# A transformer block on one core: a new head, zero products where TensorE is quiet, reordered waits, and a tail by TensorE transposes

## The chip, the cores and the metric

The kernel runs on one core of one Trainium2 chip. The metric is the device time of one execution, in microseconds (us). Before the change the median was 841.53 us (837.78 to 842.52, four runs). A time in a trace is measured from the start of the profiled execution, whose span is about 2 us shorter than its device time (843.0 us against 844.83 before).

Engines, by the profile's names: PE is TensorE (PEld its weight loads), DVE is VectorE, ACT is ScalarE, POOL is GpSimd, SP is SyncE; SPq lines are DMA issues. PEclk is the granted TensorE clock, 1.00 being full speed.

## The reference

A pre-norm block on 2048 tokens of width 640, in bf16: multi-query attention with 32 heads of width 20 that share one key and one value head, then a gated GELU feed-forward of width 1536.

```python
h  = x + softmax((LN(x) @ wq) @ (LN(x) @ wk).T * 20**-0.5) @ (LN(x) @ wv) @ wo   # 32 heads, one k and v
h2 = h + (gelu(LN(h) @ w_gate) * (LN(h) @ w_up)) @ w_down
```

The costly part is 32 x 2048 x 2048 exponentials. The kernel deals with them in 2048 score banks of 128 x 512.

## The kernel before

Everything is recorded by a planner in Python: tasks have estimated costs and latencies, and at each moment the planner gives each engine something to do. What it decides becomes a fixed order of instructions on every engine, with semaphore waits between engines. A number in the planner changes the order of instructions; it does not change what one instruction does. Both kernels are planned this way, so a small edit can reorder everything after it.

The parts that the argument touches (cut; `...` marks cuts):

```python
# waits of one instruction: DMAs first, then engines, in no order of time
ws = dmas + [v[1] for v in best.values()]
...
# GpSimd at the start, in this fixed order; the LayerNorm powers come after all of it
pool(memset wk4 ...); pool(memset wq_pad[0:4] ...); pool(wk4 copy ...)
for g in range(4): wq_copy(g)          # waits for the first half of wq
... v_ext memsets, ident, memset wq_pad[4:8]
for g in range(4, 8): wq_copy(g)       # waits for the second half of wq
...
# a LayerNorm tile is transposed by DMA, issued by SP
sp_tasks.append(_Task(("sp",), lambda e: e.dma_start_transpose(o, xn_tmp[:, s, :]), 1330, 1500, ...))
...
# the late weight loads (wo, wg, wu, wd): lowest priority, free to go from 30 us of planned time
sp_tasks.append(_Task(("sp",), ... e.dma_start(o[:], cview(v)) ..., [], [nm], 9.0, None,
                      lambda: plan.free["sp"] > 30000.0))
...
# every product has two forms: whole, or split in four pieces of 32 columns
def fn(e, b, mode):
    if mode == "m":
        return e.matmul(o(b), l, r, start=st, stop=sp)
    for j in range(4):
        a = slice(32 * j, 32 * j + 32)
        ins = e.matmul(o(b)[a, :], l[:, a], r, start=st, stop=sp, tile_position=(0, 32 * j))
...
# whole only when no attention unit is open any more
md = "m" if state["qk_left"] == 0 and not open_units() else "v"
...
# PE's choice: PV products go first only under pressure for buffers
if can_v and press:
    return do_pv()
```

A "pack" below is one set of four score products (one key tile for one attention unit); there are 512, and each feeds four score banks. ACT turns most of them into exponentials; DVE does about a quarter by integer arithmetic (545 of the 2048 banks in the profile of before).

The softmax here doesn't subtract the row's maximum and nothing guards it: scores larger than these inputs give would overflow.

Of the kernel before, what the change touches and what calls it, by code (L numbers as in the profile page):

```python
# [9 lines left out]
P = 128  # L10
_DEBUG = {}
# [27 lines left out]
class _Plan:  # L39
# [51 lines left out]
    def resolve(self):  # L91
# [6 lines left out]
        while left:  # L98
            moved = False
            for e in self.ENGINES:  # L100
                while pos[e] < len(self.ops[e]):
# [15 lines left out]
                    for d in need:  # L117
                        if d.dma:
                            dmas.append(d)
                        elif d.idx > best.get(d.eng, (-1, None))[0]:  # L120
                            best[d.eng] = (d.idx, d)
                    ws = dmas + [v[1] for v in best.values()]
                    for d in ws:
# [69 lines left out]
def bass_sequential_preLN__grouped_kv_mqa__glu_gated_geglu__prompt_kernel(  # L193
# [32 lines left out]
    BATCH_COL = [0, 256, 0, 256, 0, 256, 0, 256, 384]  # L226
    LN2G = CHUNKS
    NA = 16
    ND = 8
# [34 lines left out]
    halfc = sb("halfc", [P, 4], BF16)  # L264
    warm = sb("warm", [P, 4], BF16)
    shifts = sb("shifts", [P, 2], I32)
    xn_tmp = sb("xn_tmp", [P, NXT, D], BF16)
# [21 lines left out]
    plan = _Plan()  # L289
    G_ALL = [("g", fc, q) for fc in range(NFC) for q in range(4)]  # L290

# [5 lines left out]

    def c_pe(n, mode):
        return max(n / 2.4, 54.0) + 3.0 if mode == "m" else max(n / 2.4, 90.0) + 9.0

# [7 lines left out]
    ADD_MIN = 1  # L308
    PVF = 4
    PRA = 3  # L310
    PRD = 1
    TH0 = 2500.0
# [3 lines left out]
    MISCMAX = 1500.0  # L316
    L_PE, L_ACT, L_DVE, L_POOL = 250.0, 165.0, 150.0, 100.0

# [18 lines left out]

    pool(lambda e: e.memset(warm[:], 0.0), 80, writes=["warm"])
    pool(lambda e: e.memset(halfc[:], 0.5), 80, writes=["halfc"])
    for w in (1, 2):  # L340
        pool((lambda w: lambda e: e.memset(shifts[:, w - 1:w], CH_SHIFT[w] * 65537))(w), 80, writes=["shifts"])
    pool(lambda e: e.memset(wk4[:].bitcast(F32), 0.0), 330, writes=["wk4z"])
    pool(lambda e: e.memset(wq_pad[:, 0:4, :, :].bitcast(F32), 0.0), 1150, writes=[("wqz", 0)])
    wk4v = wk4[:].rearrange("p c (r e) -> p c r e", r=4)[:, :, :, 0:Dh]
    pool(lambda e: e.tensor_copy(wk4v, wk_sb[:].unsqueeze(2).to_broadcast([P, NC_D, 4, Dh])), 400,
         reads=["wk"], writes=["wk4", "wk4z"])

    def wq_copy(g):
        o = wq_pad[:, g, :, :].rearrange("p c (r e) -> p c r e", r=4)[:, :, :, 0:Dh]
        i = wq_stage[:, :, 4 * Dh * g:4 * Dh * (g + 1)].rearrange("p c (r e) -> p c r e", r=4)  # L350
        pool(lambda e: e.tensor_copy(o, i), 400, reads=[("wqs", g // 4), ("wqz", g // 4)] + G_ALL,
             writes=[("wqp", g)])

    for g in range(4):
        wq_copy(g)
    for w in range(3):
        pool((lambda w: lambda e: e.memset(v_ext[:, :, w, Dh:32], CH_W[w]))(w), 230,
             writes=[("vone", w)])
    plan.commit("act", lambda e: e.activation(warm[:, 0:1], warm[:, 1:2], ACT.Exp), 1500, L_ACT,
# [21 lines left out]

    def ln_stats(ln, t, prio, then):
        key = ("x", t) if ln == 0 else ("h", t)

        def b(op):
            dve(lambda e: e.bn_stats(stats[:, ln, t, 6:12], xh[:, t, HALF:D]), 356, [key], [("st", ln, t, 1)],
                prio, c)

        def c(op):
            dve(lambda e: e.bn_aggr(mv[:, ln, t, :], stats[:, ln, t, :]), 126,  # L390
                [("st", ln, t, 0), ("st", ln, t, 1)], [("mv", ln, t)], prio, then)

        dve(lambda e: e.bn_stats(stats[:, ln, t, 0:6], xh[:, t, 0:HALF]), 356, [key], [("st", ln, t, 0)], prio, b)  # L393

    def ln_group(ln, tiles, prio, done):
# [27 lines left out]
        def norm(t):  # L423
# [9 lines left out]
            def then(op):  # L433
                s = slot[0]

                def tdone(op2):
                    slots["xt"].append(s)
                    done(t, op2)

                if ln == 0:  # L440
                    o = xn1T[:, :, t * P:(t + 1) * P]
                    wkeys = [("xn1T", t)]
                else:
                    o = xn2T[:, :, xcol[t]:xcol[t] + P]
                    wkeys = [("xn2T", xcol[t])]
                def free():
                    return ln == 0 or batch_of[t] < 2 or up_left[batch_of[t] - 2] == 0

                sp_tasks.append(_Task(("sp",), lambda e: e.dma_start_transpose(o, xn_tmp[:, s, :]), 1330, 1500,
                                      [("xt", s)], wkeys, prio, tdone, free))  # L450

            key = ("x", t) if ln == 0 else ("h", t)
            tk = _Task(("dve",), None, 302, L_DVE, [key, ("lr", kk)], [], prio, then, gate)

# [8 lines left out]

        for t in tiles:
            ln_stats(ln, t, prio, after_stats)

# [21 lines left out]
    def mm(o, l, r, st, sp):  # L488

        def fn(e, b, mode):  # L490
# [6 lines left out]
            return ins  # L497
        return fn

    def kv_job(tiles):  # L500
# [157 lines left out]
    def on_transpose(t):  # L658
# [11 lines left out]
        tk.born = bind  # L670
        tk.then = lambda op: wo_job(t, sl[0], 0)
        sp_tasks.append(tk)

    def wo_job(t, s, h):
# [5 lines left out]
        def then(b):  # L680
            if h == 1:
                slots["onT"].append(s)
            else:
                wo_job(t, s, 1)

            def fin(op):
                free_bank(b)
                if h == 1:
                    h_ready(t)
            dve(lambda e: e.tensor_tensor(xh[:, t, h * HALF:(h + 1) * HALF], xh[:, t, h * HALF:(h + 1) * HALF],  # L690
                                          bank(b, HALF), ALU.add), c_dve(HALF), [("b", b), ("x", t)],
                [("hh1", t, h), ("h", t)], 1.0, fin)
        jobs.append(_Job(("wo", t, h), 2.0, pieces, then))

    h_done = set()

    def h_ready(t):
        h_done.add(t)
        for gl in LN2G:
            if t in gl and all(x in h_done for x in gl):  # L700
                ln_group(1, gl, 4.0 if t < 12 else 1.5, x2_done)

# [21 lines left out]

    def g_free(b):

        mine = set(gkeys(b, 0))
        return all(down_left[x] == 0 for x in range(b) if mine & set(gkeys(x, 0)))
# [88 lines left out]
    def down_job(b, t, h):  # L817
# [4 lines left out]
        def then(bk):  # L822
# [4 lines left out]
            def fin(op):  # L827
                free_bank(bk)
                if h == 1:
# [3 lines left out]
                                          bank(bk, HALF), ALU.add), c_dve(HALF),  # L833
                [("b", bk), ("h", t)], [("o", t, h)], 1.0, fin)
        jobs.append(_Job(("down", t, h), 3.0, pieces, then))
# [11 lines left out]
    for i, gl in enumerate([[0], [1], [2, 3], [4, 5], [6, 7], [8, 9], [10, 11], [12, 13], [14, 15]]):  # L847
        ln_group(0, gl, 2.0 + 0.01 * i, ln1_done)
    for u in units:
        q_job(u)  # L850

    pool(lambda e: e.memset(ident[:], 0.0), 120, writes=["ident0"])
    pool(lambda e: e.affine_select(out=ident[:], in_=ident[:], compare_op=ALU.not_equal, fill=1.0, base=0,
                                   pattern=[[-1, P]], channel_multiplier=1), 320, ["ident0"], ["ident"])
    pool(lambda e: e.memset(wq_pad[:, 4:8, :, :].bitcast(F32), 0.0), 1150, writes=[("wqz", 1)])
    for g in range(4, 8):
        wq_copy(g)
    for nm, o, v in (("wo", wo_sb, A_wo), ("wg", wg_sb, B_w_gate), ("wu", wu_sb, B_w_up), ("wd", wd_sb, B_w_down)):
        sp_tasks.append(_Task(("sp",), (lambda o, v: lambda e: e.dma_start(o[:], cview(v)))(o, v), 1500, 12000,
# [255 lines left out]
    def pe_decide(t):  # L1115
# [30 lines left out]
        def fits(c):  # L1146
            return t + c <= lim
# [13 lines left out]
        can_v = nr >= 1 and (fits(220.0 + swv) or press)  # L1161
        can_m = piece is not None and fits(c_pe(piece[1][1], "v") + swv)
        if can_v and press:
            return do_pv()
# [6 lines left out]
        if can_v:  # L1171
            return do_pv()
        return False

    def next_piece(t):
# [52 lines left out]
    def issue_piece(t, jb, pc):  # L1228
# [10 lines left out]
        fn = pc[0]  # L1239
        md = "m" if state["qk_left"] == 0 and not open_units() else "v"  # L1240
        sw = pe_sw(t, md)
# [82 lines left out]
    def do_adds(t, eng, w, most):  # L1324
# [7 lines left out]
        a = slice(s0 * 512, (s0 + k) * 512)  # L1332
        cost, lat = (k * 512 / 3.84 + 72.0, L_DVE) if eng == "dve" else (POOL_ADD, L_POOL)
        if eng == "dve":
            def fn(e):
                return e.tensor_scalar(pd[:, w, a], pd[:, 0, a], float(CH_SHIFT[w]), None, ALU.add)  # L1336
        else:
# [3 lines left out]
            def fn(e):  # L1341
                return e.tensor_tensor(pd32[:, w, h], pd32[:, 0, h],
                                       shifts[:, w - 1:w].to_broadcast([P, 256 * k]), ALU.add)
        op = plan.commit(eng, fn, cost, lat, [("pd", 0, s0 + i) for i in range(k)] + ["shifts"], [("pd", w, s0 + i) for i in range(k)], at=t)
        for x in recs:
            x["add"](w, op)

    def dve_decide(t):
# [52 lines left out]
        if n and pend[w][0]["at"] <= t + 20:  # L1401
# [3 lines left out]
            if n >= 4 or pd_free.count(True) < 3:  # L1405
                pr = 0.2
            if n >= ADD_MIN:
                opts.append((pr, len(opts), None))
# [19 lines left out]

    def pool_decide(t):
        for tk in tasks:  # L1430
            if tk.engs[0] == "pool" and known(tk) and plan.ready("pool", tk.reads, tk.writes) <= t + 20:
                tasks.remove(tk)
                run_task(t, tk, "pool")
                return True
        if POOL_ADD:
# [55 lines left out]
    _DEBUG["end"] = max(op.vis for e in plan.ENGINES for op in plan.ops[e])  # L1491
    _DEBUG["plan"] = plan

    plan.resolve()
# [74 lines left out]
```

## Time and profile before

| | before |
|---|---|
| device time, median | 841.53 us |
| span of the profiled run (another run, of 844.83 us) | 843.0 us |
| first exponential on ACT starts | 24.25 us |
| last exponential ends | 799.28 us |
| tail after it | 43.7 us |

The page's chain of waits that ended last, by line (the beginning is what is used here):

```profile
ACT pa L1301 63%; DVE pd L1364 4%; PE ps L1072 4%; PE ps L993 4%; PE ps L496 4%; DMA xn1T<-xn_tmp 2%; ACT gbuf L797 2%; DVE pd L1336 2%; PE ps L492 1%; DMA onT<-onq 1%; DMA xh<-in_A_x_dram 1%; ACT L1301 1%; ACT L797 1%; DVE stats L393 1%; D
```

ACT's exponentials (line L1301) are 63% of the chain. The stretches view says where they are not the limit. Its columns: the stretch, its length, then for each engine the busy us and (x) instructions, the granted clock, the DMA share and GB/s.

```profile
core 0: us, PE busy (x) PEld busy (x) DVE busy (x) ACT busy (x) POOL busy (x), PEclk, DMA share, GB/s
0.00:24.00 24.00, 4.00 (x120) 3.15 (x120) 16.03 (x65) 2.44 (x5) 13.39 (x34) 1.00 0.71 179
24.00:60.00 36.00, 25.50 (x704) 13.44 (x700) 26.22 (x82) 25.96 (x37) 6.81 (x18) 0.91 0.92 240
60.00:200.00 140.00, 107.74 (x1613) 40.71 (x1609) 128.58 (x330) 134.60 (x191) 0.71 (x1) 0.93 0.04 6
200.00:760.00 560.00, 501.85 (x9679) 233.96 (x9683) 529.50 (x1353) 551.00 (x765) 4.58 (x6) 0.96 0.06 13
799.00:843.00 44.00, 28.59 (x763) 24.13 (x752) 10.89 (x24) 5.74 (x9) 0.56 (x1) 0.92 0.09 25
```

ACT does almost nothing in the first 24 us and the last 44 us, is busy 25.96 of 36 us from 24 to 60, and 134.60 of 140 and 551.00 of 560 us in the bulk. So there are three limits: a head, a bulk bound by ACT with some 15 us of idleness left, and a tail.

Lines of the timeline in the head of before (start us, length us, engine, line, operation, out<-in, count; in brackets idle time before it and what ended it):

```profile
5.16 0.10 DVE L408 TENSOR_SCALAR ln_veb<-ln_vb 128x1 bf16<-128x1 bf16 x1
...
12.10 1.90 POOL L351 COPY wq_pad<-gbuf 128x400 bf16<-128x400 bf16 x4 [1.26 <-DMA gbuf<-in_A_wq_dram]
...
13.97 3.04 POOL L412 TENSOR_TENSOR ln_denb<-ln_veb,halfc 128x1 bf16<-128x1 bf16 x5
...
16.26 0.43 DVE L457 TENSOR_SCALAR xn_tmp<-xh,mv,ln_r 128x640 bf16<-128x640 bf16 x1
...
16.72 16.45 SPq L449 DMA_TRANSPOSE xn1T<-xn_tmp  x12
...
19.46 0.72 PE L496 MATMUL ps<-xn1T,wk 128*32 128x128 bf16 x20 [19.46 <-DMA xn1T<-xn_tmp]
...
24.25 1.94 ACT L1301 ACTIVATE pa<-ps 128x1024 bf16<-128x1024 f32 x2 [0.50 <-PE ps L993]
...
34.61 0.52 SPq L859 DMA_DIRECT2D wg_sb<-in_B_w_gate_dram  x1
38.41 7.76 SPq L449 DMA_TRANSPOSE xn1T<-xn_tmp  x4
...
49.26 1.26 PE L496 MATMUL ps<-xn1T,wk 128*32 128x256 bf16 x20 [1.53 <-DMA xn1T<-xn_tmp]
```

The variance of the first tile is ready at 5.2 us, but its power (L412, on POOL) starts at 13.97, right behind the second set of wq copies (L351). Then the normalised tile (L457), its DMA transpose (L449), and the first key product at 19.46. The last four transposes stand behind one weight load of 1.9 MB (L859), and PE's wait for the last of them ends at 49.26.

Lines of the timeline in the tail of before:

```profile
799.19 2.89 PE L496 MATMUL ps<-wd_sb,gbuf 128*32 128x320 bf16 x80
...
806.49 1.57 PE L496 MATMUL ps<-xn2T,wu_sb 128*32 128x128 bf16 x98 [1.30 <-issue]
...
809.96 0.90 PE L496 MATMUL ps<-xn2T,wg_sb 128*32 128x128 bf16 x50 [1.50 <-issue]
...
813.98 0.33 PE L496 MATMUL ps<-xn2T,wu_sb 128*32 128x128 bf16 x9 [1.70 <-issue]
...
817.51 1.21 SPq L667 DMA_TRANSPOSE onT<-onq  x1
...
820.12 1.53 PE L492 MATMUL ps<-wo_sb,onT 128*128 128x320 bf16 x10 [2.01 <-DMA onT<-onq]
...
825.07 1.21 SPq L449 DMA_TRANSPOSE xn2T<-xn_tmp  x1
...
827.77 4.45 PE L492 MATMUL ps<-xn2T,wg_sb 128*128 128x128 bf16 x40 [6.11 <-DMA xn2T<-xn_tmp]
```

Three stalls of PE are put down to "issue", that is to nothing that the profile shows waiting; they lie where PE runs long rows of 32-column pieces. Then comes the chain of the last tile, with two DMA transposes (L667, L449) that PE waits for.

### The profile page before, as it was taken

What the parts mean: (1) busy time and instruction counts of PE and PEld (TensorE: products, weight loads), DVE (VectorE), ACT (ScalarE), POOL (GpSimd) and SP (SyncE); (2) the same over time, 40 slices, a digit from 0 to 9 for tenths busy, and PEclk for the clock granted to TensorE, in tenths of its full rate; (3) what the DMA queues carried; (4) which work ended last, traced back from release to release, by engine and by line L of the source; (5) the groups of instructions that cost most, each with busy time, mean ns of one, the idle gap of its engine ahead of it and who ended that gap; (6) DMA issues with size and microseconds to landing.
All of it is one profiled execution on the core that took longest, in us unless ns stands there. A gap on an engine that the chain in (4) does not pass through costs nothing.

```text
span 843.0 us, 30901 instructions
## 1 busy us (share of the span) xinstructions
PE 703.7 (83%) x13588; PEld 333.2 (40%) x13588; DVE 748.7 (89%) x1943; ACT 758.7 (90%) x1054; POOL 26.6 (3%) x61
## 2 busy tenths in 40 slices
PE   0777768788997889988997879998998889999965
PEld 0522223243443434443443334344443434444455
DVE  7778998988999989999999899999899999999922
ACT  0769999999999999999999999999999999999910
POOL 5200000000000000000000000000000000000000
PEclk9989899998999999998999989999999999999998
DMA  6980001000010001010010000010010000010010
GB/s 185 193 237 2 2 1 18 9 11 2 3 34 17 3 2 19 19 17 3 2 34 11 9 3 18 2 34 3 2 27 10 18 2 18 10 32 5 11 34 17
DMA packets 42981, 22.68 MB, mean 27 GB/s; under 512 B 34016, under 2 KB 41568, under 8 KB 42848
## 3 DMA queue, kind: packets, MB, share of 16 engines
q1 hardware_dynamic: 40224, 19.83, 10.1%
q8 instruction: 108, 1.77, 0.9%
q10 hardware_dynamic: 2624, 0.87, 0.4%
q14 instruction: 25, 0.20, 0.1%
HBM read 10.21 MB, written 2.62 MB: 15 GB/s over the span
## 4 chain that ended last, share of the span: by engine, by line
ACT 67%; PE 13%; DVE 9%; issue 6%; DMA 5%; SPq 0%; POOLq 0%; POOL 0%
ACT pa L1301 63%; DVE pd L1364 4%; PE ps L1072 4%; PE ps L993 4%; PE ps L496 4%; DMA xn1T<-xn_tmp 2%; ACT gbuf L797 2%; DVE pd L1336 2%; PE ps L492 1%; DMA onT<-onq 1%; DMA xh<-in_A_x_dram 1%; ACT L1301 1%; ACT L797 1%; DVE stats L393 1%; DVE osb L1099 1%
## 5 line engine op out<-in xcount | busy, mean ns | idle before, releaser
L1301 ACT ACTIVATE pa<-ps 128x512 bf16<-128x512 f32 (+1 forms) x1010 | 711.9, 915 | 23.5 <-PE ps L993 21.9
L1364 DVE TENSOR_SCALAR pd<-ps 128x512 uint16<-128x512 f32 x545 | 370.6, 687 | 43.7 <-PE ps L993 32.9
L1072 PE MATMUL ps<-pd,v_ext 128*32 128x512 bf16 x1635 | 276.5, 403 | 30.2 <-ACT pa L1301 14.0
L993 PE MATMUL ps<-qT,kT 32*128 32x512 bf16 x2048 | 208.8, 395 | 61.9 <-ACT pa L1301 29.3
L1072 PE MATMUL ps<-pa,v_ext 128*32 128x512 bf16 x1503 | 253.0, 395 | 5.5 <-DVE pd L1364 2.4
L1336 DVE TENSOR_SCALAR pd<-pd 128x512 uint16<-128x512 uint16 (+2 forms) x895 | 243.8, 312 | 3.0
L993 PEld LDWEIGHTS ps<-qT,kT 32*128 32x128 bf16 x2048 | 58.1, 91 | 222.5 <-DVE pd L1364 176.3
L1072 PEld LDWEIGHTS ps<-pd,v_ext 128*32 128x32 bf16 x1635 | 72.9, 96 | 99.2 <-ACT pa L1301 28.7
L1072 PEld LDWEIGHTS ps<-pa,v_ext 128*32 128x32 bf16 x1503 | 68.4, 96 | 54.1 <-issue 28.8
L496 PE MATMUL ps<-xn2T,wu_sb 128*32 128x256 bf16 (+1 forms) x1920 | 69.6, 276 | 3.8 <-issue 3.0
L496 PE MATMUL ps<-xn2T,wg_sb 128*32 128x256 bf16 (+1 forms) x1920 | 66.5, 271 | 1.7 <-issue 1.5
L496 PE MATMUL ps<-wd_sb,gbuf 128*32 128x320 bf16 x1344 | 58.8, 300 | 0.0
L496 PEld LDWEIGHTS ps<-xn2T,wu_sb 128*32 128x32 bf16 x1920 | 46.3, 99 | 21.7 <-issue 12.6
L496 PE MATMUL ps<-xn1T,wq_pad 128*32 128x256 bf16 (+1 forms) x1440 | 52.3, 276 | 1.6 <-issue 1.1
L814 DVE TENSOR_TENSOR gbuf<-ps,gbuf 128x512 bf16<-128x512 f32 x48 | 32.8, 682 | 21.4 <-PE ps L496 10.8
L496 PEld LDWEIGHTS ps<-xn2T,wg_sb 128*32 128x32 bf16 x1920 | 44.1, 97 | 18.7 <-issue 11.9
L496 PEld LDWEIGHTS ps<-xn1T,wq_pad 128*32 128x32 bf16 x1440 | 33.9, 100 | 15.0 <-issue 8.8
L496 PEld LDWEIGHTS ps<-wd_sb,gbuf 128*32 128x32 bf16 x1344 | 32.2, 96 | 19.1 <-issue 7.5
L412 POOL TENSOR_TENSOR ln_denb<-ln_veb,halfc 128x2 bf16<-128x2 bf16 (+1 forms) x18 | 12.3, 694 | 768.2 <-DVE ln_veb L408 768.2
L777 DVE CAST gbuf<-ps 128x512 bf16<-128x512 f32 x42 | 28.6, 681 | 1.5 <-PE ps L496 1.5
L779 ACT ACTIVATE gbuf<-ps 128x512 bf16<-128x512 f32 x6 | 3.6, 597 | 28.7 <-PE ps L492 19.5
L496 PE MATMUL ps<-wo_sb,onT 128*32 128x320 bf16 x600 | 27.6, 301 | 1.0 <-DMA onT<-onq 0.8
(58 smaller groups left out, 312.6 us busy)
## 6 DMA issues: line engine op xcount, KB each, us to landing
out_dram<-xh SPq DMA_DIRECT2D x16, 160.0 KB, 1.8
xh<-in_A_x_dram SPq DMA_DIRECT2D x3, 640.0 KB, 8.8
wg_sb<-in_B_w_gate_dram SPq DMA_DIRECT2D x1, 1920.0 KB, 10.5
wu_sb<-in_B_w_up_dram SPq DMA_DIRECT2D x1, 1920.0 KB, 8.0
wd_sb<-in_B_w_down_dram SPq DMA_DIRECT2D x1, 1920.0 KB, 13.7
gbuf<-in_A_wq_dram ACTq DMA_DIRECT2D x2, 400.0 KB, 7.5
wo_sb<-in_A_wo_dram SPq DMA_DIRECT2D x1, 800.0 KB, 5.8
xh<-in_A_x_dram SPq DMA_DIRECT2D x2, 160.0 KB, 2.6
```

The costliest lines, as they stand in the source:

```text
L393: dve(lambda e: e.bn_stats(stats[:, ln, t, 0:6], xh[:, t, 0:HALF]), 356, [key], [("st", ln, t, 0)], prio, b)
L412: task(("pool",), lambda e: e.tensor_tensor(ln_denb[:, ln, sl], ln_veb[:, ln, sl], halfc[:, 0:n], ALU.pow), 1010, L_POOL, [("veb", kk), "h ...
L492: return e.matmul(o(b), l, r, start=st, stop=sp)
L496: ins = e.matmul(o(b)[a, :], l[:, a], r, start=st, stop=sp, tile_position=(0, 32 * j))
L777: dve(lambda e: e.tensor_copy(o, i), c_dve(n * k), [("b", bk)], ks, 1.0, fin)
L797: task(("act",), (lambda v: lambda e: e.activation(v, v, ACT.Gelu_apprx_tanh))(v), ("gelu", c_act(n * (f1 - f0))), L_ACT, ks, ks, 1.0, (la ...
L814: dve(lambda e: e.tensor_tensor(o, i, o, ALU.mult), c_dve(n * k), [("b", bk)] + ks, ks, 1.0, fin)
L993: ins = e.matmul(bank(b), kT4[32 * r:32 * r + 32, kt * P:(kt + 1) * P], qT[32 * r:32 * r + 32, s, :], start=True, stop=True, tile_position ...
L1072: ins = e.matmul(ps[32 * r:32 * r + 32, ab * 512:(ab + 1) * 512], v_ext[:, it["kt"], it["w"], :], it["ap"], start=st, stop=(j in ends), ti ...
L1301: op = plan.commit("act", lambda e: e.activation(dst, src, ACT.Exp, scale=SM_SCALE), cost, L_ACT, [("b", b0 + i) for i in range(n)], [("pa ...
L1336: return e.tensor_scalar(pd[:, w, a], pd[:, 0, a], float(CH_SHIFT[w]), None, ALU.add)
L1364: op = plan.commit("dve", lambda e: e.tensor_scalar(pd[:, 0, s * 512:(s + 1) * 512], bank(b), CH_A, CH_B, ALU.mult, ALU.add), c_dve(512), ...
```

## The change

Its intent, by its own words: a new head, with TensorE transposes for the first tiles and GpSimd work by urgency; zero products where TensorE is quiet; the wait that ends last placed last; a tail by TensorE transposes. The diff, cut to its core:

```diff
-                    ws = dmas + [v[1] for v in best.values()]
+                    ws = sorted(dmas + [v[1] for v in best.values()], key=lambda d: d.vis)
...
+    PE_T1 = (0, 1)      # tiles of the first LayerNorm that PE transposes
+    PE_T2 = (15,)       # of the second LayerNorm
+    PE_TO = (15,)       # of the attention output
...
-    PRD = 1
+    PRD = 2
-    L_PE, L_ACT, L_DVE, L_POOL = 250.0, 165.0, 150.0, 100.0
+    L_PE, L_ACT, L_DVE, L_POOL = 232.0, 310.0, 150.0, 100.0
...
-    (fixed order on POOL: wk4 copy, wq copies, v_ext memsets, shifts, ident)
+    (ident first; the copies and memsets become tasks with priorities, as the powers are;
+     the memset of wq_pad[4:8] moves to DVE)
...
+                if t in (PE_T1 if ln == 0 else PE_T2):
+                    tr_job(("tr", ln, t), xn_tmp[:, s, :], ("xt", s), o, wkeys, ...)   # 5 PE transposes, one ACT or DVE copy
+                    return
...
-        if can_v and press:
+        if can_v and (press or state["qk_left"] == 0):
             return do_pv()
...
+        if fits(222.0 + swv) and quiet(t):       # PE planned busy under 50% of the last 3.4 us
+            return fill(t)                       # four products of zeros (32 x 512) into the open accumulator
```

The fills add zero to an accumulator. The order of instructions, which can be built without running, holds 45 of them (180 products), mostly in the first 95 packs. It also shows that in the tail everything after the last PV products now runs in the whole form. Left out of the cut: the statistics of the second LayerNorm are now taken half tile by half tile, and the norm of the last tiles has a higher priority (0.7 instead of 1.5).

## The prediction

> What bounds it now: three stretches with different limits.
> (1) Head. In the timeline the first exponential on ScalarE (ACT) starts at 24.25 us. GpSimd works in fixed order: the first LayerNorm's variance is ready at 5.2 us, but its power starts at 13.97 us, behind eight wq copies (the last four wait for a load) and memsets. The first normalised tile is ready at 16.7 us; its DMA transpose lands 2.74 us later.
> (2) Bulk. ACT is the limit: busy 551 of 560 us from 200 to 760 us (stretches view); the chain of waits is 63% ACT exponentials. From 24 to 799 us ACT idles about 24 us: 10 before 60 us, where TensorE (PE) waits in order for the last DMA transposes among weight loads, 5 from 60 to 200, 9 after.
> (3) Tail. The last exponential ends at 799.3 us: 43.7 us of tail, PE busy only 27.6 of the last 43. From 804 to 814 us PE stalls three times for 1.3 to 1.7 us with no wait for data, about 256 PE instructions apart, in products split into 32-column pieces. [...] From 817.5 to 827.8 us runs the serial chain of the last tile, with two DMA transposes of about 2.7 us; the granted clock falls to 0.79 in 820:830.

> What the change does.
> - Head: the power goes ahead of most wq copies; tiles 0 and 1 are transposed by PE with an ACT copy (estimate 1.4 us, from 0.60 us for 512 columns, instead of 2.7). By instruction order the first norm stands behind the statistics of tiles 2 and 3 (data at 6.55 us): ready at about 9.5 us, second norm 11.5, first query product 12.5, first exponential about 16 us: 8 us earlier. PE reaches the last key products after 15 score packs instead of 11, but VectorE still norms tile 15 at about 41 us, and two transposes now queue behind two 1.9 MB weight loads, so PE waits there until about 47 us (before: 49.3). Four packs at 1.45 us plus 2 us: 7.5 us gained.
> - Bulk: same work (493 paired, 516 single exponentials against 517), 35 fewer VectorE adds (not the bottleneck). Last wait last, a later modelled ACT latency, and 180 zero products (45 sets at 0.2 to 0.4 us, mostly in the first 95 packs) can recover only part of 15 us of ACT idleness, and can delay scores: 3 us gained, give or take 5.
> - Tail: outstanding PV products go first, both units close, and the rest runs as full 128-column products (240 gate/up at 0.064 us = 15.4; 71 down at 0.137 = 9.7; wo 1.5; transposes, PV about 4). PE stays busy; two PE transposes save 1.3 us each and other work fills the chain. Last exponential to end: 32.5 us instead of 43.7, 11 us gained.

> Predicted: 841 - 7.5 - 3 - 11 = 819.5 us; range 810 to 829. Chances: faster by over 2% 0.78, within 2% 0.21, slower 0.01.

> Would show it: first exponential at 15 to 17 us; key wait until 46 to 48 us; ACT at least 98% busy in the bulk, 1.49 us per pack as before; no PE issue gaps after the last exponential, granted clock 1.0 there, tail near 32 us.

> Would make it wrong: the early lead eaten by the wait for tiles 14 and 15; zero products or the new order delaying scores; the tail chain (PV, transpose, wo, LayerNorm) exposed longer than I count; VectorE order stalling PE.

## The result, and the profile after

The changed kernel took 817.96 us (median of four, 817.45 to 822.72), before 841.53 us in the same rounds. The ratio is 0.974, 95% interval 0.969 to 0.979: faster. A ratio here is the mean time of one kernel's runs over the mean of the other's runs of the same rounds, so it is not quite the ratio of the medians. The prediction was 819.5 us, range 810 to 829.

The same stretches after:

```profile
core 0: us, PE busy (x) PEld busy (x) DVE busy (x) ACT busy (x) POOL busy (x), PEclk, DMA share, GB/s
0.00:16.60 16.60, 6.02 (x144) 4.30 (x147) 11.84 (x47) 3.85 (x8) 10.46 (x31) 1.00 0.84 229
16.60:60.00 43.40, 30.03 (x724) 14.18 (x716) 33.43 (x108) 28.92 (x40) 9.11 (x21) 0.84 0.78 203
60.00:200.00 140.00, 112.33 (x1752) 43.02 (x1750) 131.95 (x325) 137.82 (x197) 0.71 (x1) 0.98 0.03 7
200.00:760.00 560.00, 501.40 (x9919) 238.51 (x9919) 533.60 (x1353) 555.09 (x767) 4.61 (x6) 0.98 0.07 13
787.00:816.00 29.00, 25.82 (x339) 22.12 (x337) 11.26 (x24) 6.36 (x10) 0.56 (x1) 0.99 0.07 25
```

From 60 to 200 us ACT is busy 137.82 us (before 134.60), from 200 to 760 us 555.09 (before 551.00), and the granted clock is 0.98 in both (before 0.93 and 0.96). The tail lasts 28.5 us, and PE is busy 25.82 of its 29 us. The head, in lines of the timeline:

```profile
5.37 0.55 POOL L411 TENSOR_TENSOR ln_denb<-ln_veb,halfc 128x1 bf16<-128x1 bf16 x1 [1.21 <-DVE ln_veb L407]
...
9.43 0.39 DVE L460 TENSOR_SCALAR xn_tmp<-xh,mv,ln_r 128x640 bf16<-128x640 bf16 x1
...
9.88 0.71 PE L508 MATMUL ps<-ident,xn_tmp 128*128 128x128 bf16 x5 [9.88 <-DVE xn_tmp L460]
...
16.59 1.94 ACT L1375 ACTIVATE pa<-ps 128x1024 bf16<-128x1024 f32 x2 [0.83 <-PE ps L1037]
...
37.15 0.57 SPq L903 DMA_DIRECT2D wg_sb<-in_B_w_gate_dram  x1
37.77 0.56 SPq L903 DMA_DIRECT2D wu_sb<-in_B_w_up_dram  x1
40.70 7.43 SPq L452 DMA_TRANSPOSE xn1T<-xn_tmp  x2
...
52.59 0.83 PE L498 MATMUL ps<-xn1T,wk 128*32 128x256 bf16 x12 [6.58 <-DMA xn1T<-xn_tmp]
```

The power starts at 5.37 us, PE transposes the first tile (L508) at 9.88, and the first exponential starts at 16.59, 7.7 us earlier than before. But the last two DMA transposes (L452, issued from 40.70) stand behind two weight loads of 1.9 MB (L903), and PE waits 6.58 us for them, until 52.59. The tail:

```profile
787.46 1.67 PE L494 MATMUL ps<-wd_sb,gbuf 128*128 128x320 bf16 x11
...
792.21 1.52 PE L494 MATMUL ps<-wo_sb,onT 128*128 128x320 bf16 x10
...
798.04 0.44 PE L508 MATMUL ps<-ident,xn_tmp 128*128 128x128 bf16 x5
...
800.55 3.42 PE L494 MATMUL ps<-wd_sb,gbuf 128*128 128x320 bf16 x24
```

L494 is the whole form of a product; no row of PE products in the tail carries a gap put down to issue, and none waits for a DMA.

Where the time of the two profiled runs differs, read off the score products and exponentials of both timelines:

| point | before | after | ahead of before |
|---|---|---|---|
| first exponential starts | 24.25 | 16.59 | 7.7 |
| pack 15 starts (counted from 0) | 57.34 | 53.36 | 4.0 |
| pack 24 starts | 69.93 | 66.92 | 3.0 |
| pack 511 (the last) starts | 797.10 | 784.90 | 12.2 |
| last exponential ends | 799.28 | 787.08 | 12.2 |
| end | 843.0 | 815.6 | 27.4 |

So the head keeps 3.0 us of its 7.7, the bulk from pack 24 to 511 gives 9.2 (727.2 to 718.0 us), and the tail 15.2 (43.7 to 28.5). The sum is 27.4 us rather than 23.6, because the profiled run of before is one of its slower ones and the profiled run after is the fastest of its four. That run of before had a granted clock of 0.955; the 30 runs of before have 0.952 to 0.975, and the low clocks go with the long times (848.77 us at 0.952, 837.52 us at 0.975). So part of the 9.2 us belongs to that one run: against a run of before of median length the bulk would have gained nearer 6 us (an estimate, 9.2 less the 3.3 us by which 844.83 is above 841.53, if all of it lies in the bulk).

### The profile page after: what moved, and what is told of

The parts are those of the page before. It is cut to its first block, busy times and chain, and to the rows that moved or that the text cites. A ratio compares the mean times of both kernels' runs of the same rounds, so it can differ in the third digit from the quotient of the medians.

```text
span 815.6 us, 30407 instructions
## 1 busy us (share of the span) xinstructions
PE 700.5 (86%) x13361; PEld 334.7 (41%) x13361; DVE 747.1 (92%) x1913; ACT 759.0 (93%) x1055; POOL 26.0 (3%) x60
## 4 chain that ended last, share of the span: by engine, by line
ACT 67%; PE 20%; DVE 9%; DMA 3%; issue 1%; SPq 0%
ACT pa L1375 64%; PE ps L498 7%; PE ps L1037 5%; PE ps L1116 5%; DVE pd L1438 4%; PE ps L494 3%; ACT gbuf L819 2%; DVE pd L1410 2%; DMA xn1T<-xn_tmp 1%; DVE stats L391 1%; ACT L1375 1%; ACT L819 1%; DVE osb L1143 1%; DMA xh<-in_A_x_dram 1%; DMA onT<-onq 1%
## 5 line engine op out<-in xcount | busy, mean ns | idle before, releaser
L1116 PE MATMUL ps<-pd,v_ext 128*32 128x512 bf16 x1638 | 266.9, 395 | 25.9 <-DVE osb L1143 15.0
L1116 PE MATMUL ps<-pa,v_ext 128*32 128x512 bf16 x1502 | 249.2, 390 | 4.9 <-ACT pa L1375 2.0
L1410 DVE TENSOR_SCALAR pd<-pd 128x512 uint16<-128x512 uint16 (+3 forms) x860 | 239.7, 320 | 2.4
L498 PE MATMUL ps<-xn2T,wu_sb 128*32 128x256 bf16 x1680 | 64.6, 278 | 1.4 <-DVE onq L658 0.7
L498 PE MATMUL ps<-xn2T,wg_sb 128*32 128x256 bf16 x1680 | 62.6, 274 | 0.6 <-DVE onq L658 0.3
L498 PE MATMUL ps<-wd_sb,gbuf 128*32 128x320 bf16 x1252 | 55.2, 300 | 0.2 <-DVE xh L718 0.2
L498 PEld LDWEIGHTS ps<-xn2T,wu_sb 128*32 128x32 bf16 x1680 | 41.3, 97 | 19.7 <-issue 10.0
L498 PE MATMUL ps<-xn1T,wq_pad 128*32 128x256 bf16 (+1 forms) x1440 | 48.7, 266 | 0.3 <-DVE xh L718 0.2
L498 PEld LDWEIGHTS ps<-xn2T,wg_sb 128*32 128x32 bf16 x1680 | 41.3, 96 | 15.3 <-issue 10.5
L391 DVE BATCH_NORM_STATS2 stats<-xh 128x6 f32<-128x320 bf16 x64 | 29.8, 480 | 3.3 <-DMA xh<-in_A_x_dram 3.3
L799 DVE CAST gbuf<-ps 128x512 bf16<-128x512 f32 x42 | 28.6, 682 | 0.0
```

Source lines behind the costliest of these rows:

```text
L391: dve(lambda e: e.bn_stats(stats[:, ln, t, 6 * h:6 * h + 6], xh[:, t, h * HALF:(h + 1) * HALF]), 356, [key], [("st", ln, t, h)], prio, c)
L799: dve(lambda e: e.tensor_copy(o, i), c_dve(n * k), [("b", bk)], ks, 1.0, fin)
L1116: ins = e.matmul(ps[32 * r:32 * r + 32, ab * 512:(ab + 1) * 512], v_ext[:, it["kt"], it["w"], :], it["ap"], start=st, stop=(j in ends), ti ...
L1410: return e.tensor_scalar(pd[:, w, a], pd[:, 0, a], float(CH_SHIFT[w]), None, ALU.add)
```

## The experiments

The theory to test: the head's lead is lost to the order of transposes and weight loads; the bulk gains by the clock that the zero products hold up, and by the order; the tail gains because PV first makes everything whole, which takes away instruction supply stalls. Rivals: the wait order, luck of the order, and the PE transposes.

Twelve kernels ran, four to a chip, each group beside the kernel before. All gave correct results. Five (`waits_old`, `fill_tiny`, `tail_nopv`, `tail_split`, `tail_dma`) leave every instruction's place unchanged up to the point of the edit. The others replan from the head on.

| run | edit to the changed kernel | median us | ratio to before | pack 24 | pack 24 to 511 | tail |
|---|---|---|---|---|---|---|
| again | none | 818.75 | 0.971 | 69.15 | 717.1 | 28.5 |
| waits_old | waits in the old order | 815.39 | 0.967 | 68.70 | 715.1 | 28.6 |
| fill_tiny | zero products of 8 columns | 822.54 | 0.976 | 68.38 | 721.1 | 28.6 |
| null_plan | planner counts 3 ns more | 816.55 | 0.968 | 70.86 | 712.6 | 28.7 |
| tail_nopv | PV not first in the tail | 827.85 | 0.984 | 68.12 | 715.8 | 40.0 |
| tail_split | tail products split | 828.98 | 0.985 | 67.87 | 714.8 | 40.1 |
| tail_dma | last tile by DMA | 819.08 | 0.973 | 68.22 | 717.1 | 28.8 |
| gate_weights | loads after the transposes | 811.24 | 0.964 | 63.10 | 715.3 | 28.6 |
| lat_old | old latencies | 827.14 | 0.982 | 70.15 | 720.0 | 30.3 |
| t1_dma | tiles 0, 1 by DMA | 809.83 | 0.962 | 63.08 | 716.3 | 28.7 |
| pool_fixed | POOL in fixed order | 822.79 | 0.977 | 73.38 | 714.3 | 28.7 |
| gate_waits_old | gate_weights and waits_old | 810.75 | 0.962 | 60.96 | 717.2 | 28.5 |

The last three columns are of each one's profiled run. Pack 24 is the start of that pack; the tail is the span minus the end of the last exponential, good to 0.1 us. Each comparison below with the control (chip 3) is across chips for the second and third group; the ratios to before, taken on one chip, say the same. The three groups, by lines of four, ran on three chips; medians of before there were 841.57, 840.92 and 841.00 us.

| | null_plan | again | after | lat_old | fill_tiny | before |
|---|---|---|---|---|---|---|
| at half clock, us | 3.4 | 17.1 | 23.9 | 27.3 | 37.5 | 61.4 |
| pack 24 to 511, us | 712.6 | 717.1 | 718.0 | 720.0 | 721.1 | 727.2 |

A straight line of 0.25 us for each us at half clock fits all fourteen within 1.3 us. This is a correlation; only fill_tiny, below, shows cause. Five runs that have the instruction order of the changed kernel in this stretch (again, the first profiled run and the three `tail_` runs) spread from 714.8 to 718.0 us, with 10.2 to 23.9 us at half clock, so single reads of the bulk are good to about 3 us.

### again: the control

> The changed kernel itself, as the control of this group. Every theory expects 818 us (first exponential near 16.6 us, last one near 787 us, tail near 28.5 us) and a ratio to before near 0.974; its scatter says how small a difference the other runs can show.

818.17 to 820.72 us in five runs. The first exponential and the tail repeat, but pack 24 came at 69.15 us instead of 66.92: in the profiled run of the same program the wait for the late transposes ended some 2 us later. So single reads of the head are good to about 2 us.

### waits_old: the order of waits

```diff
-                    ws = sorted(dmas + [v[1] for v in best.values()], key=lambda d: d.vis)
+                    ws = dmas + [v[1] for v in best.values()]
```

> Same instructions in the same order on every engine; only the order of the waits before one instruction is put back to that of before. If putting the wait that ends last at the end is worth time (542 of 1057 waiting TensorE instructions wait for two things), the bulk from pack 24 to pack 511 (718.0 us in the changed kernel, 727.2 before) grows by 2 to 4 us. The rival, that a ScalarE which is 98% busy hides it, expects under 1 us of difference.

Neither came: the old order was not slower but 3.4 us faster by medians (814.5 to 818.98 against 818.17 to 820.72, which overlap in one of its six runs). The later pair, gate_waits_old against gate_weights, shows 0.5 us. No gain from putting the last wait last is shown in either pair. Whether it costs anything stays open.

### fill_tiny: zero products without their length

```diff
-  ins = e.matmul(ps[..., ab * 512:(ab + 1) * 512], zz[:], kT4[:, 0:512], start=False, ...)
+  ins = e.matmul(ps[..., ab * 512:ab * 512 + 8],   zz[:], kT4[:, 0:8],   start=False, ...)
```

> Same instructions, order and waits; each zero product has 8 columns instead of 512, so it hardly keeps TensorE busy. If the zero products earn by holding the granted clock, the mean clock falls from 0.977 towards the 0.955 of before, the stretch from pack 24 to 96 (100.5 us changed, 105.4 before) grows back by 3 to 5 us and the total by as much. The rival, that the bulk's gain comes from the new order and the fills do nothing, expects the same time within 1 us; a third, that the fills stand in the way of scores, expects it 1 to 3 us shorter.

822.54 us, with all five runs (821.98 to 825.34) above all five of the control: 3.8 us by medians. The stretches of the control, then of fill_tiny:

```profile
60.00:140.00 80.00, 63.33 (x938) 22.97 (x942) 74.94 (x188) 78.94 (x116) 0.00 (x0) 1.00 0.03 6
400.00:780.00 380.00, 339.61 (x6814) 162.67 (x6813) 363.99 (x916) 378.01 (x523) 4.65 (x5) 0.99 0.08 14
```

```profile
60.00:140.00 80.00, 61.45 (x910) 22.38 (x910) 72.89 (x183) 77.04 (x113) 0.00 (x0) 0.94 0.03 6
400.00:780.00 380.00, 338.58 (x6824) 162.65 (x6817) 364.05 (x917) 378.21 (x523) 4.66 (x5) 0.99 0.08 14
```

Where the fills lie, the clock falls (1.00 to 0.94 from 60 to 140 us) and ACT loses busy time (78.94 to 77.04). From 400 us on, where there are few fills, both are equal. Pack 24 to 511 grew from 717.1 to 721.1 us, and 3.3 us of that lie between packs 24 and 96 (100.5 to 103.8 us, within the expected 3 to 5). The clock theory holds: the fills are worth about 4 us, and all of it in the bulk. The mean granted clock over the profiled run was 0.966, in the control 0.981. Between 60 and 140 us fill_tiny has three stretches of 3.4 us with a granted clock of 0.50 (from 96.2, 113.2 and 123.5 us), the control none. Two long waits of PE show the clock fall while PE stands: in the head of the changed kernel PE stands from 46.01 to 52.59 us, and the clock is at half from 50.6 to 57.5; in the tail of before it stands for 6.11 us until 827.77, and the clock is at half from 825.8 to 832.6. How long a quiet stretch it takes is not shown. What a half clock costs is seen in the head of the changed kernel, where one set of four score products takes 0.61 us at 38.36 us (clock 0.50) and 0.39 us at 41.53 (clock 1.00).

### null_plan: how much a meaningless reordering moves

```diff
-            cost = c_act(512 * n)
+            cost = c_act(512 * n) + 3.0
```

> A meaningless nudge: the kernel's planner counts 3 ns more for each exponential, so the order comes out different from the head on while nothing else is changed. It measures what a different order alone does. If orders are interchangeable, the time stays within 2 us of the control; if it moves by 4 us or more, then the 9.2 us that the bulk gained can be in part luck of the order, and runs that replan from the head on cannot settle differences of that size.

816.55 us, 2.2 us under the control; pack 24 to 511 took 712.6 us, 4.4 less than the control, while pack 24 came 1.7 us later. So a replanned bulk moves by about 4 us for no reason that was meant; it goes with the clock, which was at half for 3.4 us in that stretch instead of 17.1. Differences of that size between replanned runs are not to be put down to the edit.

### tail_nopv: PV not first

```diff
-        if can_v and (press or state["qk_left"] == 0):
+        if can_v and press:
```

> Identical to the changed kernel until the last score product; then outstanding PV products no longer go before other work. The tail (last exponential to end, 28.5 us in the changed kernel, 43.7 before) should grow, as the last unit closes later and more products run split while it is open: by 3 to 8 us if PV first is a main cause of the tail's gain, by under 1 us if the full-width form and the transposes do it all.

The tail grew by 11.5 us (28.5 to 40.0), more than expected, and the total by 9.1 against the control (8.8 against tail_dma on the same chip). The stalls of before are back, three of 1.04 to 1.50 us, and the chain of the last tile is exposed again, because the attention unit stays open while split products go first. By the waits view of its tail PE stands 4.0 us at the stalls and 4.9 us before the transposes and products of that chain.

### tail_split: same order, split products

```diff
-        plan.commit("pe", lambda e: fn(e, b, md), c_pe(pc[1], md) + sw, ...)
+        plan.commit("pe", lambda e: fn(e, b, "v"), c_pe(pc[1], md) + sw, ...)
```

> Same plan, order and waits; in the tail the products of gate, up, down and wo are issued as four 32-column pieces each instead of one full product. If the stalls of 1.3 to 1.7 us every 256 TensorE instructions in the tail of before are instruction supply, they come back: about 310 full products become 1240, about 1860 more instructions with their weight loads, 7 stalls, so the tail grows by 8 to 12 us with idle time put down to issue. If those stalls came from something else, the tail grows by less than 3 us.

The tail grew by 11.6 us, in the expected range of 8 to 12, with nothing moved. The waits view of its tail puts 9.4 us of PE idleness down to issue, in eight stalls. Lines of its timeline:

```profile
809.68 0.41 PE L498 MATMUL ps<-xn2T,wu_sb 128*32 128x128 bf16 x16 [0.22 <-issue]
809.90 1.75 PE L498 MATMUL ps<-xn2T,wg_sb 128*32 128x128 bf16 x112
813.15 0.85 PE L498 MATMUL ps<-xn2T,wg_sb 128*32 128x128 bf16 x48 [1.50 <-issue]
813.82 1.30 PE L498 MATMUL ps<-xn2T,wu_sb 128*32 128x128 bf16 x80
816.62 1.30 PE L498 MATMUL ps<-xn2T,wu_sb 128*32 128x128 bf16 x80 [1.50 <-issue]
```

From the piece at 809.68 to the stall's end at 813.15 PE runs 16 + 112 = 128 products, from there to 816.62 48 + 80 = 128. Each has a weight load, so that is 256 instructions, and each time 3.47 us. In the tail of before the stalls end at 806.49 and 809.96, again 3.47 us apart. From the end of one stall to the next, no 256 instructions took less than 3.47 us here (3.47 to 4.02). The DMA records show what goes with it: queue q8, of kind instruction, moves blocks of 16 KB, and each of the eight stalls here and of the three in the tail of before ends 2.2 to 2.8 us after one of these blocks starts (at 810.88 and 814.32 us for the stalls that end at 813.15 and 816.62). Whole products show no such stall: 20 of them start every 1.12 us, so 128 take 7.2 us, and in the tail of the changed kernel the blocks start at 787.39, 796.41 and 804.86 us, over 8 us apart. That the stalls are waits for the instructions in these blocks is the reading; shown are the equal counts, the blocks before the stalls' ends, and that splitting alone brings the stalls back. The 11.6 us are the price of splitting the whole tail; before paid less of it, three stalls of 4.5 us in all, since from 814.46 us on it ran whole products too.

### tail_dma: the last tile by DMA

```diff
-    PE_T2 = (15,)
-    PE_TO = (15,)
+    PE_T2 = ()
+    PE_TO = ()
```

> Identical to the changed kernel until the tail; the two transposes of the last tile go by DMA again. Counted as a chain they cost 1.3 us more each, so up to 3 us more; if other products fill the wait (as the plan intends), under 1 us; more than 3 us if a DMA also waits behind output stores in its queue.

819.08 us and a tail of 28.8 us, against 818.75 and 28.5: nothing. PE fills the wait with other tiles' products: the waits view of its tail lists no wait of PE for a DMA (its rows go down to 0.7 us). What they are worth where the chain is exposed is not shown: tail_nopv, with PE transposes, has a tail of 40.0 us, and before, without them, one of 43.7, but these two differ in order as well.

### gate_weights: weight loads after the transposes

```diff
-     [], [nm], 9.0, None, lambda: plan.free["sp"] > 30000.0))
+     [], [nm], 9.0, None, lambda: plan.free["sp"] > 30000.0
+                                  and all(("xn1T", t) in plan.w for t in range(NT))))
```

> The three late weight loads are held back until all transposes of the first LayerNorm are issued (replans from 30 us on). In the changed kernel TensorE waits 6.6 us, until 52.6 us, for the transposes of tiles 14 and 15, which were issued behind two weight loads; the lead of 7.7 us at the first exponential is 3.0 us by pack 24. If the loads are what eats the lead, the wait shrinks to under 2 us, pack 24 comes at about 62 to 63 us instead of 66.9, and the total falls by 3 to 5 us. If VectorE's norms are what is late (tile 15 normed at 41.8 us), pack 24 moves by less than 1.5 us.

811.24 us, 7.5 us under the control by medians and 7.8 under tail_dma on the same chip. Pack 24 came at 63.10 us; the three other kernels of that group, which run the changed head, have it at 67.87 to 68.22. SP's lines and PE's last key product in gate_weights:

```profile
12.98 30.93 SPq L452 DMA_TRANSPOSE xn1T<-xn_tmp  x14
43.96 1.56 SPq L903 DMA_DIRECT2D wo_sb<-in_A_wo_dram  x1
45.57 0.53 SPq L903 DMA_DIRECT2D wg_sb<-in_B_w_gate_dram  x1
```

```profile
46.79 1.26 PE L498 MATMUL ps<-xn1T,wk 128*32 128x256 bf16 x20 [1.27 <-DMA xn1T<-xn_tmp]
```

All 14 DMA transposes go out before the first load, and PE's wait for the last is 1.27 us instead of 6.58. The longest time from a transpose's issue to its landing was 4.2 us, in the changed kernel 11.2; tile 15 is normalised no earlier than in the changed kernel (just after 41 us in both). So it is the loads and not DVE that eat the lead. In the trace of the changed kernel the two transposes issued behind 3.8 MB of loads landed just after them: the second load at 51.31 us, the transposes at 51.88 and 52.46. The pack-24 gain is about 5 us; the rest of the 7.5 lies within what replanning moves.

### lat_old: the old latencies

```diff
-    L_PE, L_ACT, L_DVE, L_POOL = 232.0, 310.0, 150.0, 100.0
+    L_PE, L_ACT, L_DVE, L_POOL = 250.0, 165.0, 150.0, 100.0
```

> The changed kernel planned with the latencies of before (TensorE 250, ScalarE 165 ns instead of 232 and 310), so another order from the head on. The zero products account for about 3 us of the bulk's gain (pack 24 to 511: before 727.2, control 717.0, tiny fills 721.3); if the later ScalarE latency is the rest, that stretch grows by 4 to 7 us against the control, beyond the 2 us that the meaningless nudge moved the total. If it is not, the total stays within 3 us of 818.

827.14 us, 8.4 us over the control's median. But in its profiled run, one of 824.59 us, pack 24 to 511 is only 3.0 us longer than in the control, below the expected 4 to 7 and within what null_plan moved by chance; pack 24 comes 1.0 us later and the tail is 1.8 us longer. The total says that in this change the new latencies gave a better order than the old ones, by more than the 2.2 us of the nudge. One nudge does not bound what another order can do by chance (t1_dma, next, moves the total by 8.9 us through an accident of the order), so it is not shown that the latencies themselves are the cause, nor that the bulk's remaining gain is theirs.

### t1_dma: no PE transposes in the head

```diff
-    PE_T1 = (0, 1)
+    PE_T1 = ()
```

> Tiles 0 and 1 are transposed by DMA again. The first exponential moves from 16.6 us to 18.5 to 20 us (a DMA transpose took 2.7 us against 1.6 on TensorE with the copy, and two in a row 1.3 more). If the wait for tiles 14 and 15 swallows the head's lead, pack 24 stays within 67 to 69.5 us and the total within 2 us of 818; if the lead reaches the end, the total grows by 2 to 4 us.

A miss. The first exponential moved to 19.25 us as expected (control 16.81), but the total fell to 809.83 us, 8.9 under the control. In this plan all 16 transposes happen to be issued by 38.06 us, before the first load; pack 24 comes at 63.08 us, as in gate_weights. So this run is in the main the gate again by another road, though not a clean repeat: VectorE's norm of tile 15 also starts earlier, at 33.86 us instead of 41.39. It shows that the PE transposes of the first tiles start the exponentials about 2.4 us earlier. With the loads out of the way a kernel without them ends no later than one with them (809.83 against 811.24 us for gate_weights); as the two plans differ, what these transposes alone are worth is not isolated.

### pool_fixed: GpSimd in fixed order

```diff
     def ptask(fn, cost, reads, writes, prio):
-        task(("pool",), fn, cost, L_POOL, reads, writes, prio)
+        pool(fn, cost, reads, writes)
```

> GpSimd does the key copy, all eight wq copies and the memsets in fixed order before the first power, as in before. The first power then starts near 14 us instead of 5.4, the first exponential near 22 to 24 us (before: 24.25). If the head's lead is only worth what pack 24 shows, the total grows by 3 us (to about 821); if the wait for tiles 14 and 15 swallows all of it, by under 1.5 us; if the lead were kept in full, by 6 to 7 us.

822.79 us, 4.0 over the control. The first power starts late again:

```profile
15.46 3.05 POOL L411 TENSOR_TENSOR ln_denb<-ln_veb,halfc 128x1 bf16<-128x1 bf16 x5
```

The first exponential starts at 22.94 us and pack 24 at 73.38, 4.2 us after the control. PE's wait for the late transposes ends at about the same time in both (54.80 and 55.08 us), but fewer packs are done before it: 12 instead of 15. So GpSimd's order is worth about 4 us in total of the 6.1 that it gains at the first exponential (16.81 against 22.94). That is nearer to the first of the three guesses (3 us) than to the others, and it suggests that about 4 us of the head's lead do reach the end. As the run replans, this is good to a few us only: its profiled run, the fastest of the four, is just 1.6 us over the control's, because its bulk came out 2.8 us shorter.

### gate_waits_old: the two faster edits together

> The two edits that came out faster than the changed kernel together: weight loads held back until the transposes are issued, and the waits in the order of before (same instruction order as the gated kernel, which gave 811.2 us and a ratio of 0.964). If the old wait order is truly worth 2 to 3 us (815.4 against 818.75), this gives 808 to 809.5 us; if that difference was chance, 811 us. Either way it should be the fastest, about 4% under before.

810.75 us (809.65 to 811.08, six runs), a ratio of 0.962 to before; gate_weights alone gave 811.24. The wait order adds nothing clear. gate_weights, t1_dma and gate_waits_old (809.8 to 811.2 us) all beat both kernels, and among themselves they are the same.

## Why the prediction was right

The total was right (819.5 predicted, 817.96 measured), the class too, and each of the three parts gained. But the terms of the sum were off, and their errors partly cancelled.

1. Head start: right. The first exponential was forecast at about 16 us and came at 16.59; the first norm at 9.5 us and came at 9.43 to 9.82. The order of instructions of the changed kernel gave this, not the diff. pool_fixed shows that GpSimd's order does most of it.
2. Head lead, predicted as "7.5 us gained": mis-sized; 3.0 us were left at pack 24 in the first profiled run, and in the control even less. The mechanism (two transposes behind two loads) was named, and "the early lead eaten by the wait for tiles 14 and 15" stood among what would make it wrong, but the wait was taken to end at "about 47 us" and it ended at 52.59, later than the 49.3 of before. With that one number put in, the prediction's own sum gives 2.5 us (four packs at 1.45, less 3.3). gate_weights confirms the cause.
3. Bulk, "3 us gained, give or take 5": mis-sized; it measured 9.2, or nearer 6 against a run of before of median length, which lies within the stated give or take. fill_tiny shows about 4 us of it to be the clock that the zero products hold. The prediction named the granted clock in the tail only (0.79); from 60 to 200 us it was 0.93, and from pack 24 to 511 before spent 61.4 us at half clock, the changed kernel 23.9. At 0.25 us each these 37.5 us go with all of the 9.2. What brought about the part of it that the fills did not, whether the latencies, the wait order, PRD or luck of the order, is not settled; null_plan shows that some 4 us can be luck, and no run isolates PRD.
4. Tail, "32.5 us instead of 43.7, 11 us gained": the mechanism was right and shown by tail_split and tail_nopv, but mis-sized; it measured 28.5, a gain of 15.2. Two terms are mis-sized. One is "240 gate/up at 0.064 us": 0.064 is 1.28 us for a row of 20 divided by 20, but the row's length includes the end of its last product; rows follow each other every 1.12 us, 0.056 us each, so 13.4 us instead of 15.4. The other is "transposes, PV about 4": the three rows of transposes take about 0.8 us of PE until the next row starts, and the PV products were done 0.4 us after the last exponential (the first whole product starts at 787.46), so about 1.2 us instead of 4. Where the 15.2 us lie is read from the tail of before, where PE stood 4.5 us at the three stalls and 8.1 us before the products that waited for the last tile's two DMA transposes (2.01 and 6.11); neither is left in the changed kernel.
5. "Two PE transposes save 1.3 us each": nothing of it in this order, as tail_dma shows; the other half of the same sentence, that other work fills the chain, is why.

## What to carry to other kernels

Ask of every early lead which wait comes next: 7.7 us at the first exponential became 3.0 because the next wait hung on small urgent transfers issued behind large idle ones (up to 11.2 us from a transpose's issue to its landing behind two loads of 1.9 MB, at most 4.2 us with the loads held back). The loads could wait, and a gate of one line was worth more (about 7.5 us of the total, of which about 5 us are read in the head) than GpSimd's new order (4.0 us, by pool_fixed).
Useless work in the gaps of a quiet engine can pay when its clock falls without it: here 180 zero products held TensorE's granted clock at 1.00 instead of 0.94 from 60 to 140 us and were worth about 4 us. Rows of many small instructions stalled here without any engine or semaphore showing why (eight stalls, 9.4 us in the tail of tail_split): look for gaps put down to issue at equal instruction counts (256 here, at least 3.47 us from the end of one stall to the next).
Before crediting a few us to a scheduler's parameter, run a meaningless nudge of it, and read the granted clock of the stretch beside its time.
